# Weights times values with the values stationary in the two column halves of TensorE, weights normalized before the transposes, and all scores in native float32

## Chip, core and metric

The kernel runs on one NeuronCore of one Trainium2 chip. The metric is device time in microseconds (us) of one execution. TensorE (PE) multiplies, VectorE (DVE) and ScalarE (ACT) do everything that is done element by element, GpSimd (POOL) prepares a few constants, and SyncE (SP) issues the loads and stores. PEld is the row of the profile for the loading of stationary operands into PE.

## What is computed

Local attention with a few global keys, then two feed-forward layers on its result:

```python
scores = scale * np.matmul(q, k.transpose(0, 1, 3, 2))        # batch 2, heads 8, seq 768, head_dim 64
is_global = pos[None, :] < int(n_global)                      # n_global 8
is_local = (rel >= 0) & (rel < int(n_local))                  # n_local 96
scores = np.where(keep, scores + bias, -1000000000.0)         # bias: -slope of the head * distance
a = np.exp(scores - np.max(scores, axis=-1, keepdims=True))
a = a / (np.sum(a, axis=-1, keepdims=True) + 1e-09)
x = np.matmul(a, v)                                           # to 1536 tokens x 512
x = moe(x)     # h = x @ w_in (512 x 2048), ELU of h, @ w_out (2048 x 512)
return moe2(x) # the same sizes, h * sigmoid(1.702 h)
```

## The kernel before

**Rows and units.** The 1536 tokens are 12 rows of 128 queries, 6 in each batch. A row is worked in two units of 4 heads, so there are 24 units. The queries of a row look at one block of 128 keys (the first row of a batch) or at two: its own block, and the block before it, whose first 32 keys are overwritten with the first 32 keys of the batch, so that the global keys lie there (`load_va` for the values, the copies at the end of the scores in `unit` for the keys).

**One unit** (`Band.unit`, lines 585 to 735) runs so:
- Scores on PE (L627), head pairs in the two row halves of the array, since a head has 64 dimensions. Rows 0 to 3 are native float32 (`NNAT = 4`; row 0's are issued at L281). From row 4 on q and k are split into a high and a low part of a shorter float (`prep`, L555: two copies and two subtractions of 128x512 each row), and three matmuls hi*hi, hi*lo, lo*hi add up to a score block. From row 4 on the scores of both units are made at once (`WHOLE = 4`).
- DVE adds the distance and takes the row's extreme (L658), ACT takes exp in place (L662) into `E`.
- PE transposes the 4 blocks (one a head and key block) of `E` (L675), and ACT or DVE copies them to `pt` (L681).
- PE multiplies: `pt` is stationary (128 keys x 128 queries), `v` with two further columns of ones is streamed (66 columns, L692). So `ob` holds, with queries on the partitions, 64 values and the sum of the weights.
- DVE adds 1e-9 to the sums (L703), takes reciprocals (L705) and scales (L707) into `o`.
- PE transposes `o` back (L718), so that features are on the partitions, into `xb`. After the second unit ACT and DVE write the row's `xh` (L731) and `xl` (L734), the split input of the first layer.

**The layers** (`FFN`) work in 8 groups of 4 blocks of 128 hidden units, for each of 3 chunks of 512 tokens: `A` (L397, first product, then the activation on ACT and DVE and a split into `g`), `B` (L437, second product, added to `acc` or `d`). Each product is three matmuls of split operands, too. `conv` turns the weights, which arrive as float32, into split operands (L362 to L374). The first group's first chunk is worked as two halves of 256 tokens, so that it can start when rows 0 and 1 are done.

**What sets the order.** `Plan` is a list scheduler that runs when the program is built. Every step is a node with a due time, the engines that it can run on with a planned cost, and the buffers it reads and writes. `TIMES` sets the due times of the units, `LEAD`, `CONV0` and `CONVS` those of the layers and conversions. Steps with two possible engines are given to the one that is planned to end first. Where PE is planned to be idle before 45 us, `idle` puts matmuls on zeros of 256 columns there (L747), "fill" from here on. There are 8 banks of PSUM, allotted by the plan too.

**The beginning** (`start`, `load`): SP loads the two sizes `n_raw`, then q and k of row 0 in two halves, row 1, and v of row 0. `NWARM = 8` matmuls of 512 zero columns run on PE meanwhile (L278).

Of the kernel before, what the change touches and what calls it, by code (L numbers as in the profile page):

```python
# [19 lines left out]
NB = S // 128  # L20
# [7 lines left out]
LEAD = 9.86  # L28
CONV0 = (-15.923, 4.66)
CONVS = (-57.99, -6.01)  # L30
TIMES = (8.0, 3.97, 3.55)
NWARM = 8
START = dict(PE=6.3, ACT=5.4, DVE=5.6, POOL=5.9, SP=5.9)
WARM = 5.0
SLOW = 8.0
ROW0 = 5.6, 6.3
PEEK = 0.58, 3.0
FILL = 45.0
NNAT = 4
WHOLE = 4  # L40
NGBUF = 5
# [4 lines left out]
VW = D + 2  # L46
# [20 lines left out]
class Node:  # L67
    __slots__ = ("due", "opts", "npred", "succ", "ready", "alloc", "uses")
# [13 lines left out]
class Plan:  # L82
# [18 lines left out]
    def node(self, due, opts, reads=(), writes=(), alloc=None, uses=()):  # L101
        n = Node()
        alloc = [] if alloc is None else alloc if isinstance(alloc, list) else [alloc]
        n.due, n.opts, n.alloc, n.uses = due, opts, alloc, uses
# [144 lines left out]
def start(k, ns, load):  # L249
# [12 lines left out]
    V.memset(f32(k.zero), 0.0)  # L262
    rel, neg = (k.e[0][:, x:x + 256] for x in (0, 256))
# [5 lines left out]
                   allow_small_or_imprecise_dtypes=True)  # L269
    k.ident = cp.tile([128, 128], F32, name="ident")  # L270
    make_identity(nc, k.ident)
    for t in k.v + k.va:
        nc.gpsimd.memset(t[:, :, D:VW], 1.0)
# [9 lines left out]
    small = lambda n, nm, dt=F32: cp.tile([128, n], dt, name=nm)  # L283
# [7 lines left out]
    V.tensor_scalar(a[:, 0:1], k.ng, float(NGLOB), None, ALU.is_le)  # L291
    V.tensor_scalar(a[:, 1:2], k.nl, float(NWIN + 1), None, ALU.is_le)
    V.tensor_scalar(k.big, col, k.ng, BIG, ALU.is_ge, ALU.mult)
    V.scalar_tensor_tensor(c, k.nl, 1.0, a[:, 1:2], ALU.is_ge, ALU.mult)
    V.scalar_tensor_tensor(w, rel[:, 128:256], k.nl, k.big, ALU.is_ge, ALU.mult)
    V.tensor_tensor(flag, c, a[:, 0:1], ALU.mult)
# [8 lines left out]
class FFN:  # L305
# [23 lines left out]
    def gbuf(self, i):  # L329
        if i < 4:  # L330
            return [(self.k.g[:, 2 * i + x, :], [("g", i, x)]) for x in range(2)]
        return [(self.k.q[1][x].rearrange("p a b -> p (a b)"), [("q", 1, x)]) for x in range(2)]
# [43 lines left out]
    def A(self, due, G, c, f, t0=0, n=TC):  # L376
# [6 lines left out]
        i = self.nA % 4 if self.nA < 12 else self.nA % NGBUF  # L383
# [115 lines left out]
class Band:  # L499
# [6 lines left out]
    def __init__(self, k, plan, pool):  # L506
# [3 lines left out]
        self.E = k.E  # L510
        self.pt = [t([128, 512], F32, f"pt{i}") for i in range(4)]
        self.o = [t([128, 512], F32, f"o{i}") for i in range(2)]
# [23 lines left out]
    def load(self, r, due):  # L536
        k, node = self.k, self.plan.node
        p = r % 2
        if r < 2:
            self.plan.given((4.9, 7.6)[r], ("acc", 0, r), *(("kn", pr, r) for pr in range(NP)))  # L540
        if r == 0:
            self.plan.given(9.3, ("v", 0))
# [3 lines left out]
        elif r >= NNAT:  # L546
            node(due, [("SP", 0.33, lambda: k.load_qk(r), 1.7)], writes=["rqk"])
        if r > 0:
            node(due + 0.1, [("SP", 0.6, lambda: k.load_v(r, self.v[p][:, :, 0:D]), 1.4)],
                 writes=[("v", p)])  # L550
        if r % NB:
            node(due + 0.2, [("SP", 1.3, lambda: k.load_va(r, self.va[p][:, :, 0:D]), 1.4)],
                 writes=[("va", p)])

    def prep(self, r, due):  # L555

        k, nc, node = self.k, self.k.nc, self.plan.node
        i = r % NB
        pos, p = POS[i], r % 2
        if r < NNAT:  # L560
            return
        if r == NNAT:
            for a, b, x in ((0, NGLOB, 0), (NGLOB, 128, 3)):
                src = k.kn[:, x, :, a:b]
                h, l = (k.kT[:, y, :, a:b] for y in range(2))
                n = NP * (b - a)
                kn = [("kn", pr, x) for pr in range(NP)]
                key = [[("kT", y, pr, 0) for pr in range(NP)] for y in range(2)]
                x = node(due - 2, o_copy(k, h, src, n), kn, key[0])
                x.ready = dict.fromkeys(ENGINES, 20.0)  # L570
                node(due - 1.5, o_sub(k, l, src, f32(h), n), kn + key[0], key[1])
        qh, ql = k.q[p]
        node(due, o_copy(k, qh, k.rqk[:, 0], 512), ["rqk"], [("q", p, 0)])
        node(due + 0.5, o_sub(k, ql, k.rqk[:, 0], f32(qh), 512), ["rqk", ("q", p, 0)], [("q", p, 1)])
        kb = lambda x, ps: [("kT", x, pr, ps) for pr in range(NP)]
        kh, kl = (k.kT[:, x, :, pos * 128:(pos + 1) * 128] for x in range(2))
        node(due + 0.2, o_copy(k, kh, k.rqk[:, 1], 512), ["rqk"], kb(0, pos))
        node(due + 1, o_sub(k, kl, k.rqk[:, 1], f32(kh), 512), ["rqk"] + kb(0, pos), kb(1, pos))
        if i == 3:
            for x in range(2):  # L580
                node(due + 1.5, o_copy(k, k.kT[:, x, :, 32:128],
                                       f32(k.kT[:, x, :, 3 * 128 + 32:4 * 128]), 384),
                     kb(x, 3), kb(x, 0))

    def unit(self, u, due):
# [6 lines left out]
        pos = POS[i]  # L592
        c0 = (pos + 1) * 128 - W
        q = k.q[p]
# [4 lines left out]
        native = r < NNAT  # L599
# [397 lines left out]
```

## Time and profile before

| | us |
|---|---|
| median of 3 runs | 623.6 (623.06 to 623.67) |
| the profiled execution | 623.17 |
| its span, first to last instruction | 621.4 |
| PE busy in the span | 614.6 (99%), 3257 records |
| DVE busy | 407.1 (66%) |
| ACT busy | 319.3 (51%) |
| granted TensorE clock, mean | 0.999 of full speed |

1.8 us of the profiled execution lie around the span. "Busy" is the time in which an engine has an instruction under way; on PE, where matmuls are pipelined and their ends are modelled, the distance from one start to the next says more of what a matmul costs, and the timeline of PE shows it: a line of the timeline is a run of like instructions, with the start of the first. A native float32 matmul leaves two records in the trace, any other one.

### The profile page before, as it was taken

To read this page: it belongs to the slowest core of one execution; us is meant where nothing else is said; L and a number is where in the kernel's file an instruction comes from. 1 tells how busy PE (TensorE), PEld (TensorE's weight loads), DVE (VectorE), ACT (ScalarE), POOL (GpSimd) and SP (SyncE) were. 2 spreads that over 40 slices of the span, in tenths; PEclk is the share of its full clock that TensorE was granted. 3 is DMA by queue.
4 is the path that set the end of the run, shared out by engine and by line. 5 is a ranking of instruction groups with operands and counts; after the bars stand their busy time and mean duration, and the time that the engine had idled before them with its cause. 6 is when DMAs were issued, how large, how long until landed. Compare 5 with 4: busy or idle time off the path is not lost.

```text
span 621.4 us, 8504 instructions
## 1 busy us (share of the span) xinstructions
PE 614.6 (99%) x3257; PEld 520.9 (84%) x3257; DVE 407.1 (66%) x873; ACT 319.3 (51%) x612; POOL 1.4 (0%) x12
## 2 busy tenths in 40 slices
PE   8999999999999999999999999999999999999997
PEld 6899998888888888888888888888888888888886
DVE  7999996737844687459856984188347954654433
ACT  6998887846724653444654654356115422521320
POOL 0000000000000000000000000000000000000000
PEclk9999999999999999999999999999999999999999
DMA  7766461212310032012210221023101310101012
GB/s 220 233 183 214 119 190 35 55 49 69 136 69 0 35 135 103 0 35 102 102 34 1 102 101 69 1 102 136 35 0 69 135 69 0 35 0 52 17 69 73
DMA packets 36833, 49.39 MB, mean 79 GB/s; under 512 B 24624, under 2 KB 25392, under 8 KB 36784
## 3 DMA queue, kind: packets, MB, share of 16 engines
q1 hardware_dynamic: 36784, 48.77, 24.2%
q8 instruction: 27, 0.44, 0.3%
q14 instruction: 22, 0.18, 0.1%
HBM read 45.62 MB, written 3.15 MB: 78 GB/s over the span
## 4 chain that ended last, share of the span: by engine, by line
PE 98%; DMA 1%; SPq 0%; DVE 0%; issue 0%
PE bank L397 42%; PE bank L437 42%; PE bank L692 6%; PE bank L675 3%; PE bank L627 3%; DMA acc<-in_qk_dram 1%; PE bank L718 1%; SPq L904 0%; DVE d L458 0%; SPq L259 0%
## 5 line engine op out<-in xcount | busy, mean ns | idle before, releaser
L397 PE MATMUL bank<-xh,wbig 128*128 128x512 f32 (+1 forms) x560 | 174.6, 381 | 0.0
L397 PEld LDWEIGHTS bank<-xh,wbig 128*128 128x128 f32 x560 | 103.9, 188 | 18.7
L397 PE MATMUL bank<-xl,wbig 128*128 128x512 f32 (+1 forms) x280 | 105.5, 377 | 0.0
L437 PE MATMUL bank<-g,wbig 128*128 128x512 f32 (+1 forms) x420 | 96.8, 369 | 0.0
L437 PEld LDWEIGHTS bank<-g,wbig 128*128 128x128 f32 x420 | 73.1, 188 | 12.4
L397 PE MATMUL bank<-xh,kT 128*128 128x512 f32 x240 | 76.3, 389 | 0.0
L241 DVE TENSOR_TENSOR g<-gt,g 128x512 fp32r<-128x512 f32 (+1 forms) x82 | 54.5, 665 | 26.2 <-ACT g L234 24.9
L234 ACT ACTIVATE g<-gt 128x512 fp32r<-128x512 f32 (+1 forms) x82 | 50.1, 611 | 40.8 <-DVE gt L415 24.9
L437 PE MATMUL bank<-wbig,g 128*128 128x512 f32 (+1 forms) x267 | 67.5, 387 | 0.0
L458 DVE SCALAR_TENSOR_TENSOR acc<-bank,acc 128x512 f32<-128x512 f32 x48 | 33.2, 692 | 52.2 <-PE bank L437 52.0
L413 ACT ACTIVATE e<-bank 128x512 f32<-128x512 f32 x48 | 28.6, 597 | 69.4 <-PE bank L397 69.1
L397 PEld LDWEIGHTS bank<-xl,wbig 128*128 128x128 f32 x280 | 52.7, 188 | 9.1
L437 PEld LDWEIGHTS bank<-wbig,g 128*128 128x128 f32 x267 | 49.8, 188 | 10.2
L234 ACT ACTIVATE wbig<-m 128x512 fp32r<-128x512 f32 x41 | 26.0, 634 | 59.8 <-PE bank L397 36.4
L397 PEld LDWEIGHTS bank<-xh,kT 128*128 128x128 f32 x240 | 45.0, 188 | 9.3
L415 DVE SCALAR_TENSOR_TENSOR gt<-e,bank 128x512 f32<-128x512 f32 x48 | 32.9, 685 | 29.7 <-ACT e L413 29.4
L437 PE MATMUL bank<-kT,g 128*128 128x512 f32 (+1 forms) x198 | 49.6, 383 | 0.0
L364 ACT ACTIVATE m<-raw 128x512 f32<-128x512 f32 x61 | 40.6, 666 | 12.5 <-DMA raw<-in_w2i_dram 6.2
L397 PE MATMUL bank<-xl,kT 128*128 128x512 f32 x120 | 46.7, 389 | 0.0
L410 DVE SCALAR_TENSOR_TENSOR gt<-e,bank 128x512 f32<-128x512 f32 (+1 forms) x52 | 33.5, 644 | 17.8 <-ACT e L408 16.9
L371 DVE SCALAR_TENSOR_TENSOR m<-m,raw 128x512 int32<-128x512 int32 x64 | 44.0, 688 | 0.8
L369 DVE SCALAR_TENSOR_TENSOR raw<-raw 128x512 int32<-128x512 int32 x64 | 44.0, 688 | 0.6
(118 smaller groups left out, 858.8 us busy)
## 6 DMA issues: line engine op xcount, KB each, us to landing
raw<-in_w1i_dram SPq DMA_DIRECT2D x16, 512.0 KB, 3.3
raw<-in_w1o_dram SPq DMA_DIRECT2D x16, 512.0 KB, 3.2
raw<-in_w2i_dram SPq DMA_DIRECT2D x16, 512.0 KB, 3.2
raw<-in_w2o_dram SPq DMA_DIRECT2D x16, 512.0 KB, 3.2
rqk<-in_qk_dram SPq DMA_DIRECT2D x8, 512.0 KB, 4.2
v<-in_v_dram SPq DMA_DIRECT2D x12, 256.0 KB, 3.9
out_dram<-acc SPq DMA_DIRECT2D x8, 256.0 KB, 2.0
va<-in_v_dram SPq DMA_DIRECT2D x10, 192.0 KB, 4.3
```

The source lines that it names most:

```text
L234: ("ACT", n / 1200 + (0.05 if psum else 0.09), lambda: nc.scalar.activation(out, in_, AF.Copy)),
L241: return [("DVE", n / 960 + 0.068, lambda: nc.vector.tensor_tensor(out, a, b, ALU.subtract))]
L364: ("ACT", 0.52, lambda: nc.scalar.activation(mf, topf, AF.Copy, scale=sc)),
L369: node(due + 1, [("DVE", 0.6, lambda: V.scalar_tensor_tensor(top, bot, 29, top, ALU.logical_shift_right, ALU.bitwise_or))], [kr], [kr])
L371: node(due + 1.5, [("DVE", 0.6, lambda: V.scalar_tensor_tensor(m, m, 3, top, ALU.logical_shift_left, ALU.bitwise_or))], [km, kr], [km])
L397: nc.tensor.matmul(h(), lhsT=w[:, kk, :], rhs=x[:, kk, :], start=(kk == 0 and j == 0), stop=(kk == KK - 1 and j == 2))
L410: node(due + 1, [("DVE", n / 960 + 0.07, lambda: V.scalar_tensor_tensor(gt, e, -1.0, h(), ALU.add, ALU.max))], [ke, b], [kg], uses=[b])
L413: node(due, [("ACT", n / 1200 + 0.05, lambda: S.activation(e, h(), AF.Tanh, scale=0.851))], [b], [ke], uses=[b])
L415: node(due + 1, [("DVE", n / 960 + 0.07, lambda: V.scalar_tensor_tensor(gt, e, 1.0, h(), ALU.add, ALU.mult))], [ke, b], [kg], uses=[b])
L437: nc.tensor.matmul(o(), lhsT=lhsT, rhs=rhs, start=(f == 0 and j == 0), stop=(f == GF - 1 and j == 2))
L458: node(due, [("DVE", n / 960 + 0.07, lambda: V.scalar_tensor_tensor(acc, o(), sc, acc, ALU.mult, ALU.add))], [b] + ka, ka, uses=[b])
L692: nc.tensor.matmul(ob.tile[:, n * VW:(n + 1) * VW], lhsT=pt[:, (hd * nw + ch) * 128:(hd * nw + ch + 1) * 128], rhs=v[:, 4 * half + n, :], ...
```

## The change

- **Weights times values:** `v` (64 columns of a head) is stationary, `pt` (128 queries) is streamed. Head 0 of a pair goes to the left 64 columns of the array and partitions 0 to 63 of PSUM, head 1 to the right half and partitions 64 to 127. The result has the features on the partitions and goes to `xb` at once; the transposes of `o`, `o` itself and the two columns of ones in `v` are gone.
- **Sums and normalization:** exp on ACT also gives the sum (`accum_out`). DVE adds 1e-9, takes reciprocals, and scales the four blocks of `E` before they are transposed.
- **Scores:** all rows are native float32, in matmuls of 128 columns for each key block (rows 1 to 3 had 256 columns). `prep` is gone; q and k of rows 4 to 11 lie in three buffers `qk`. Rows 4 to 7 make their scores unit by unit now (`WHOLE = 8`).
- **The beginning:** the halves of rows 0 and 1 are issued on the ACT and SP queues, 6 zero matmuls instead of 8, the flag that picks the program is worked out earlier.
- **The plan:** other due times and costs, a reserve of PSUM banks (`spare`), six `g` buffers instead of five.

```diff
-LEAD = 9.86
-CONV0 = (-15.923, 4.66)
-CONVS = (-57.99, -6.01)
-TIMES = (8.0, 3.97, 3.55)
-NWARM = 8
+LEAD = 13.8
+CONV0 = (-12.46, 4.78)
+CONVS = (-57.99, -1.63)
+TIMES = (8.0, 4.6, 3.75)
+NWARM = 6
...
-WHOLE = 4
-NGBUF = 5
+WHOLE = 8
+NGBUF = 6
...
-                    self.banks) >= len(n.alloc) else 1e9
+                    self.banks) >= len(n.alloc) + n.spare else 1e9
...
-    for t in k.v + k.va:
-        nc.gpsimd.memset(t[:, :, D:VW], 1.0)
...
             def mm():
                 for y, pr in enumerate(ps):
-                    js = slice(y % 2 * W, (y % 2 + 1) * W)
-                    for n, (a, x) in enumerate(parts):
+                    for w, (keys, _) in enumerate(blocks):
+                        js = slice(y % 2 * W + w * 128, y % 2 * W + w * 128 + 128)
                         for hd in range(2):
                             rows = slice(64 * hd, 64 * hd + 64)
-                            rhs = (k.kn[rows, pos + 1 - nw:pos + 1, pr, :] if native
-                                   else x[rows, pr, c0:c0 + W])
-                            nc.tensor.matmul(own[y // 2 * 2 + hd].tile[:, js], lhsT=a[rows, pr, :],
-                                             rhs=rhs, start=(n == 0), stop=(n == len(parts) - 1))
+                            nc.tensor.matmul(own[y // 2 * 2 + hd].tile[:, js], lhsT=q[rows, pr, :],
+                                             rhs=keys[rows, pr, :], start=True, stop=True)
...
-                node(at + 0.5, [("ACT", W / 1200 + 0.19, lambda n=n, e=e: nc.scalar.activation(
-                    e, e, AF.Exp, bias=st[:, n:n + 1], scale=-1.0))],
-                    [(kE, n), (kst, n)], [(kE, n)])
-        ob = Bank()
+                node(at + 0.5, [("ACT", W / 1200 + 0.28, lambda n=n, e=e: nc.scalar.activation(
+                    e, e, AF.Exp, bias=st[:, n:n + 1], scale=-1.0, accum_out=st[:, 4 + n:5 + n]))],
+                    [(kE, n), (kst, n)], [(kE, n), (kst, 4 + n)])
+        node(due + 2.1, [("DVE", 0.17, lambda: V.tensor_scalar(
+            st[:, 8:12], st[:, 4:8], 1e-9, None, ALU.add))],
+            [(kst, 4 + n) for n in range(4)], [(kst, 8)])
+        node(due + 2.2, [("DVE", 0.1, lambda: V.reciprocal(st[:, 12:16], st[:, 8:12]))],
+             [(kst, 8)], [(kst, 12)])
+        for n in range(4):
+            e = E[:, n, 0:W]
+            node(due + 2.3, o_ts(k, e, e, st[:, 12 + n:13 + n], 1.0, ALU.mult, ALU.mult, W),
+                 [(kE, n), (kst, 12)], [(kE, n)])
...
             def pv(j=j, pt=pt):
-                for hd in range(2):
-                    n = 2 * j + hd
-                    for ch in range(nw):
-                        v = self.v[p] if ch == nw - 1 else self.va[p]
+                pr = 2 * half + j
+                for ch in range(nw):
+                    v = self.v[p] if ch == nw - 1 else self.va[p]
+                    for hd in range(2):
                         nc.tensor.matmul(
-                            ob.tile[:, n * VW:(n + 1) * VW],
-                            lhsT=pt[:, (hd * nw + ch) * 128:(hd * nw + ch + 1) * 128],
-                            rhs=v[:, 4 * half + n, :], start=(ch == 0), stop=(ch == nw - 1))
+                            xb.tile[64 * hd:64 * hd + 64, pr * 128:(pr + 1) * 128],
+                            lhsT=v[:, 2 * pr + hd, :],
+                            rhs=pt[:, (hd * nw + ch) * 128:(hd * nw + ch + 1) * 128],
+                            start=(ch == 0), stop=(ch == nw - 1))
...
-        def ot():
-            for j in range(2):
-                n = 2 * half + j
-                nc.tensor.transpose(xb.tile[:, n * 128:(n + 1) * 128], o[:, n * 128:(n + 1) * 128],
-                                    k.ident)
...
     def load():
-        load_early(0, 2)
-        load_early(1)
-        load_v(0, k.v[0][:, :, 0:D])
+        for r in range(2):
+            load_early(r, (nc.scalar, nc.sync))
+        load_v(0, k.v[0])
```

**How rows move.** Names are buffers with a number; L692 and L718 of before are the product and the transposes of `o`, L664 of the change is the product, L675 and L647 are the transposes of `E`, L627 and L596 the scores, L747 and L697 the fill matmuls. On PE in the middle of the third row (two key blocks), before:

```order
L627 MATMUL bank_70<-acc 128x256
L692 MATMUL bank_68<-va_104,pt_180 128x66
L692 MATMUL bank_68<-v_102,pt_180 128x66
L692 MATMUL bank_68<-va_104,pt_180 128x66
L692 MATMUL bank_68<-v_102,pt_180 128x66
L718 MATMUL bank_71<-ident,o_182 128x128 x2
L692 MATMUL bank_68<-va_104,pt_181 128x66
```

and with the change, in the second row:

```order
L596 MATMUL bank_68<-acc 128x128
L664 MATMUL bank_66<-pt_177,va_105 64x128 x2
L664 MATMUL bank_66<-pt_177,v_103 64x128 x2
L664 MATMUL bank_66<-pt_178,va_105 64x128 x2
L664 MATMUL bank_66<-pt_178,v_103 64x128 x2
L647 MATMUL bank_73<-ident,E_99 128x128 x4
L647 MATMUL bank_69<-ident,E_99 128x128 x4
L697 MATMUL bank_67<-q1h 128x256 x5
```

The transposes of `o` between the products are gone, two heads stand in one row as a pair of matmuls (x2), and fill matmuls have come in.

On PE at the beginning, from the first fill matmul on, before:

```order
L747 MATMUL bank_70<-q1h 128x256 x5
L627 MATMUL bank_70<-acc 128x256
L627 MATMUL bank_71<-acc 128x256
L627 MATMUL bank_70<-acc 128x256
L627 MATMUL bank_71<-acc 128x256
L675 MATMUL bank_72<-ident,E_99 128x128 x2
```

and with the change, behind row 1's scores, of which the last is the first row here:

```order
L596 MATMUL bank_73<-acc 128x128
L697 MATMUL bank_66<-q1h 128x256 x7
L647 MATMUL bank_66<-ident,E_99 128x128 x2
L647 MATMUL bank_67<-ident,E_99 128x128 x2
L697 MATMUL bank_69<-q1h 128x256 x3
L664 MATMUL bank_69<-pt_177,v_102 64x128 x2
L664 MATMUL bank_69<-pt_178,v_102 64x128 x2
L697 MATMUL bank_68<-q1h 128x256 x20
```

Both units' scores of row 1 stand ahead of the first transposes, and in all there are 40 fill matmuls where there were 5.

On DVE at the end of the second unit, before (the sums come out of PSUM, L703, and the scaled result goes to `o`, L707):

```order
L703 TENSOR_SCALAR st_185<-bank_70 128x4
L705 RECIPROCAL st_185<-st_185 128x4
L707 TENSOR_TENSOR o_182<-bank_70,st_185 128x256
L367 TENSOR_SCALAR raw_90<-raw_90 128x512
L369 SCALAR_TENSOR_TENSOR raw_90<-raw_90 128x512
```

and with the change, at the third unit (L626 to L629 sums and reciprocals, L245 the scaling of `E`, L619 the scores' minimum):

```order
L626 TENSOR_SCALAR st_183<-st_183 128x4
L629 RECIPROCAL st_183<-st_183 128x4
L234 COPY acc<-acc 128x2x32
L245 TENSOR_SCALAR E_101<-E_101,st_183 128x256 x4
L619 ISA E_100,st_182<-bank_68,d 128x256
```

The normalization stands ahead of the transposes now, and takes four instructions of 256 columns instead of one.

## Rows read from the trace of the kernel before

**Rows 1.** The page: busy time by engine, and the chain that ended last.

```profile
PE 614.6 (99%) x3257; PEld 520.9 (84%) x3257; DVE 407.1 (66%) x873; ACT 319.3 (51%) x612; POOL 1.4 (0%) x12
...
PE 98%; DMA 1%; SPq 0%; DVE 0%; issue 0%
```

**Rows 2.** Windows: length, busy us (instructions) of PE, PEld, DVE, ACT, POOL; clock; DMA.

```profile
16.00:32.00 16.00, 16.00 (x139) 14.28 (x138) 15.90 (x53) 15.79 (x38) 0.00 (x0) 1.00 0.75 226
32.00:48.00 16.00, 16.00 (x150) 15.57 (x149) 15.80 (x56) 16.00 (x40) 0.00 (x0) 1.00 0.70 198
...
64.00:80.00 16.00, 16.00 (x163) 15.56 (x162) 14.55 (x61) 13.09 (x37) 0.00 (x0) 1.00 0.40 116
...
200.00:400.00 200.00, 200.00 (x884) 165.62 (x883) 131.98 (x211) 101.30 (x168) 0.00 (x0) 1.00 0.18 64
```

**Rows 3.** Groups by shape on PE: the products and the transposes of `o`.

```profile
L692 PE MATMUL bank<-v,pt 128*128 128x66 f32 x192 | 35.0, 275 | 0.0
L692 PE MATMUL bank<-va,pt 128*128 128x66 f32 x160 | 29.8, 268 | 0.0
...
L718 PE MATMUL bank<-ident,o 128*128 128x128 f32 x48 | 9.5, 279 | 0.0
```

**Rows 4.** Timeline of PE, rows 2 and 3: start, us, line, tiles, shape, count.

```profile
17.25 2.00 PE L627 MATMUL bank<-acc 64*128 64x256 f32 x16
19.18 0.44 PE L718 MATMUL bank<-ident,o 128*128 128x128 f32 x2
...
22.02 0.60 PE L675 MATMUL bank<-ident,E 128*128 128x128 f32 x4
22.55 1.13 PE L627 MATMUL bank<-acc 64*128 64x256 f32 x8
23.61 0.44 PE L692 MATMUL bank<-va,pt 128*128 128x66 f32 x2
...
24.33 0.39 PE L692 MATMUL bank<-v,pt 128*128 128x66 f32 x2
24.56 0.39 PE L718 MATMUL bank<-ident,o 128*128 128x128 f32 x2
24.78 0.34 PE L692 MATMUL bank<-va,pt 128*128 128x66 f32 x2
```

**Rows 5.** Timeline of PE: split scores of row 4, 24 matmuls between these starts.

```profile
37.01 0.50 PE L627 MATMUL bank<-kT,q0h 64*128 64x256 f32 x4
...
38.63 0.66 PE L675 MATMUL bank<-ident,E 128*128 128x128 f32 x4
```

**Rows 6.** Timelines of PE at the beginning, three windows; in brackets idle before.

```profile
5.84 0.72 PE L281 MATMUL bank<-acc 64*128 64x128 f32 x10
...
6.07 0.50 PE L281 MATMUL bank<-acc 64*128 64x128 f32 x6
...
6.49 0.86 PE L747 MATMUL bank<-q1h 128*128 128x256 f32 x5
8.62 1.14 PE L627 MATMUL bank<-acc 64*128 64x256 f32 x8 [1.26 <-DMA acc<-in_qk_dram]
```

**Rows 7.** Timeline of DVE: scaling, subtraction of a split, and the score step.

```profile
7.87 0.89 DVE L246 TENSOR_SCALAR d<-gt 128x256 f32<-128x256 f32 x4
8.68 0.28 DVE L658 CUSTOM_DVE_ANT_0 E<-bank,E 128x128 f32<-128x128 f32 x1
...
17.91 0.69 DVE L241 TENSOR_TENSOR wbig<-m,wbig 128x512 fp32r<-128x512 f32 x1
18.51 0.42 DVE L707 TENSOR_TENSOR o<-bank,st 128x256 f32<-128x256 f32 x1
18.85 0.42 DVE L658 CUSTOM_DVE_ANT_0 E<-bank,d 128x256 f32<-128x256 f32 x1
```

**Rows 8.** Groups by shape on DVE: reading out an accumulator.

```profile
L658 DVE DVE_READ_ACCUMULATOR2_ANT st<- 128x1 f32 x96 | 8.0, 83 | 0.0
```

More of the change, by code (lines that the diff above doesn't have):

```diff
@@ L27 @@
 NSLOT = 6
-LEAD = 9.86
-CONV0 = (-15.923, 4.66)
-CONVS = (-57.99, -6.01)
-TIMES = (8.0, 3.97, 3.55)
-NWARM = 8
-START = dict(PE=6.3, ACT=5.4, DVE=5.6, POOL=5.9, SP=5.9)
+LEAD = 13.8
[3 more added lines that the diff above has]
+NWARM = 6
+START = dict(PE=5.8, ACT=5.1, DVE=5.9, POOL=5.9, SP=5.6)
 WARM = 5.0
 SLOW = 8.0
-ROW0 = 5.6, 6.3
-PEEK = 0.58, 3.0
+ROW0 = 5.2, 5.8
+PEEK = 0.47, 3.0
 FILL = 45.0
 NNAT = 4
-WHOLE = 4
-NGBUF = 5
+WHOLE = 8
+NGBUF = 6
 NG = DFF // 128 // GF
@@ L331, in gbuf @@
             return [(self.k.g[:, 2 * i + x, :], [("g", i, x)]) for x in range(2)]
-        return [(self.k.q[1][x].rearrange("p a b -> p (a b)"), [("q", 1, x)]) for x in range(2)]
+        return [(self.k.q[i - 4][x].rearrange("p a b -> p (a b)"), [("q", i - 4, x)])
+                for x in range(2)]
     def acc(self, c, m):
@@ L510, in __init__ @@
         self.E = k.E
+        k.qk = [k.rqk] + [t([128, 2, NP, 128], F32, f"qk{i}") for i in range(1, 3)]
         self.pt = [t([128, 512], F32, f"pt{i}") for i in range(4)]
[L512 removed]
         self.st = [t([128, 16], F32, f"st{i}") for i in range(3)]
@@ L539, in load @@
         if r < 2:
-            self.plan.given((4.9, 7.6)[r], ("acc", 0, r), *(("kn", pr, r) for pr in range(NP)))
+            self.plan.given((4.4, 6.0)[r], ("acc", 0, r), *(("kn", pr, r) for pr in range(NP)))
         if r == 0:
-            self.plan.given(9.3, ("v", 0))
+            self.plan.given(8.8, ("v", 0))
+            self.plan.given(5.35, "d0")
         if 1 < r < NNAT:
@@ L553, in load, with keys @@
                  writes=[("va", p)])
[L555 to L559, printed above, removed]
+    def keys(self, r):
+        k = self.k
         if r < NNAT:
[L561 to L583, printed above, removed]
@@ L585, in unit @@
+            return k.kn[:, r], [("kn", pr, r) for pr in range(NP)]
+        return k.qk[r % 3][:, 1], [("k", r % 3, pr) for pr in range(NP)]
     def unit(self, u, due):
@@ L619, in mm @@
+            blocks = [self.keys(x) for x in range(r + 1 - nw, r + 1)]
+            kk = [kq] + [names[pr] for _, names in blocks for pr in ps]
             def mm():
                 for y, pr in enumerate(ps):
-                    js = slice(y % 2 * W, (y % 2 + 1) * W)
-                    for n, (a, x) in enumerate(parts):
+                    for w, (keys, _) in enumerate(blocks):
+                        js = slice(y % 2 * W + w * 128, y % 2 * W + w * 128 + 128)
                         for hd in range(2):
@@ L896, in tile_local_attention_two_ffn, with load_qk, load_early @@
     k.rqk = t([128, 2, NP, 128], F32, "rqk")
-    def load_qk(r):
-        nc.sync.dma_start(out=k.rqk, in_=qk[r])
-    def load_early(r, n=1):
-        w = 512 // n
-        for c in (slice(j * w, j * w + w) for j in range(n)):
-            nc.sync.dma_start(out=k.acc[:, r::NNAT, c],
-                              in_=qk[r].rearrange("p x a b -> p x (a b)")[:, :, c])
+    def load_qk(r, to=None):
+        nc.sync.dma_start(out=k.rqk if to is None else to, in_=qk[r])
+    def load_early(r, queues=(nc.sync,)):
+        w = 512 // len(queues)
+        for j, queue in enumerate(queues):
+            c = slice(j * w, j * w + w)
+            queue.dma_start(out=k.acc[:, r::NNAT, c],
+                            in_=qk[r].rearrange("p x a b -> p x (a b)")[:, :, c])
     heads = lambda a: a.rearrange("p (h d) -> p h d", d=D)
```

90 lines of the change are left out of this document (30 added, 60 removed).

## Prediction

> **What bounds the kernel now.** I read the page first: PE is busy for 99% of the span, and the chain that ended last runs over PE for 98% [rows 1]. That alone proves little, since a busy PE need not be a dense one, so I then read the timeline of PE for the distances between starts. They are constant: every two records of the product take 0.22 to 0.23 us, also where another line follows [rows 4]. Only ahead of the first scores of row 1 is there a wait, 1.26 us for their load [rows 6]. The windows say what would come next: from 16 to 48 us DVE and ACT are as full as PE (15.9 and 15.8 of 16, then 15.8 and 16.0), from 64 us on both have slack, and in the layers, 200 to 400 us, DVE is busy 132 of 200 us and PE 200 [rows 2]. So a microsecond taken off PE is a microsecond of the end, except in about the first 70 us, where DVE and ACT may not let PE run ahead.
>
> The sum is made against the profiled execution, 623.2 us; the median of the runs is 0.4 us above it, less than I can resolve.
>
> **The products, the large term.** A float32 matmul leaves two records; 192 and 160 records [rows 3] are 176 matmuls. A record takes 0.112 us from start to start (24.33 to 24.56) [rows 4], so the products take 352 x 0.112 = 39.4 us. A record streams 66 columns there, but a transpose of 128 columns takes the same 0.11 (24.56 to 24.78, two of them), so it isn't the streaming that sets the pace; both load 128 stationary columns. With the change a record streams 128 columns and loads 64. No row shows two matmuls in the two column halves. The nearest show two in the row halves, float32 as well: 10 records from 5.84 on and 6 from 6.07 on, so 4 records or two pairs in 0.23 us [rows 6], 0.115 a pair at 128 columns; at 256 columns 16 records take 1.93 us with what follows, 8 take 1.06 [rows 4], so four pairs take 0.87, 0.109 for each 128 columns. Were the two row halves not at work at once, a pair would take twice that. So the bounds for a pair of records in the column halves are 0.112 (at once) and 0.223 (one after the other). I take 0.112, from the row halves: 176 x 0.112 = 19.7 us, a gain of **19.7 us**; the other end is no gain.
>
> **The change of array shape.** Going into and out of the row halves costs time: of the 1.06 us of four pairs 0.87 are streaming, so 0.19 is not; and four transposes ahead of them take 0.53 us (22.02 to 22.55) where four take 4 x 0.11 = 0.44 [rows 4]. Together 0.28 us a group. By the order the products stand in 27 groups, with other work between. Whether the column halves cost this too no row shows; bounds 0 and 0.28. I take 0.28, the only row of such a change: **+7.6 us**; the other end is 0. The Trainium skill says that changing the tiling mode drains TensorE (TensorEngine Tiling (Array Packing), Key Properties); the 0.28 us of the row halves agree with it, and by the rule the column halves would pay as well, so 615; without it 607.
>
> **The transposes of o** go: 48 [rows 3] at 0.11 us: **-5.3 us**.
>
> **The scores.** Row 4's 24 split matmuls take 38.63 - 37.01 = 1.62 us [rows 5]. Native in 128 columns they are 16 pairs of records: 16 x 0.112 + 0.28 = 2.07 us. Rows 8 to 11: 4 x 0.45 = 1.8. Rows 4, 5 and 7 make two groups each: 2 x (0.90 + 0.28) - 1.62 = 0.74, so 2.2. Row 6 (one key block) and rows 1 to 3 (8 pairs of 128 columns for 4 of 256, the same streaming) I put at 0.3 together. Sum **+4.3 us**.
>
> **The beginning.** Row 1 is issued on two queues and lands earlier: the wait of 1.26 us [rows 6] can go. Two zero matmuls fewer, but the load of row 0 sets that start: I take 0.4 (0 to 0.9). Sum **-1.7 us**.
>
> **Idle PE early.** Before the first layer has work, PE has rows 0 to 3 only, and DVE and ACT are full there [rows 2]. Per unit of two key blocks the change adds four scalings, 0.2 us each (four in 0.81, 7.87 to 8.68), and takes away one of 0.34 (18.51 to 18.85) [rows 7]; ACT gets four sums to read out, for which the nearest row is DVE's accumulator, 0.083 us each [rows 8], where it hides nearly all behind the next instruction; bounds 0 and 0.2. For rows 0 to 3: 24 x 0.2 + 8 x 0.13 + 32 x 0.08 - 8 x 0.34 = 5.7 us on two engines that were full, about 3 us each, while PE loses work. For rows 4 to 6 the split of q and k goes, two subtractions of 0.60 (17.91 to 18.51) [rows 7] and two copies, about 2.1 us a row, which pays for the scalings there. So PE must wait early. How much, the order says in part: 40 fill matmuls where 5 stood, 35 x 0.12 = **+4.2 us**; for 256 columns in one record I take the pace of the split scores, (1.62 - 0.28) / 12 = 0.11 us a pair [rows 5], rounded up. Beyond the fill I put **+2 us** for waits on DVE and ACT up to row 6 (0 to 7). Later both have room (64 to 80) [rows 2], and what was hidden stays so. Loads of v as plain rows, the three qk buffers, POOL's constants and the sixth g buffer cost nothing: no wait on them but the one of 1.26 us ends on PE.
>
> **Sum:** -19.7 + 7.6 - 5.3 + 4.3 - 1.7 + 4.2 + 2.0 = -8.6, so 623.2 - 8.6 = 614.6. I say **614.5 us**.
>
> **Rivals.**
> 1. *DVE and ACT bind the first 70 us.* If the sums cost ACT 0.2 us each, 56 of them up to row 6 cost 11 us instead of 4.6, and the chain of each unit (four exps, sum, reciprocal, scalings, only then transposes) leaves holes on two full engines: waits of 7 instead of 2 us, **619.5 us** (618 to 623). For it: [rows 2]; against it: the split of rows 4 to 6 leaves the same engines.
> 2. *The column halves don't run at once.* Then the product keeps 0.223 us a pair: no 19.7, and all other terms stay but the 2 us of waits, since PE is slower: -5.3 + 4.3 + 7.6 - 1.7 + 4.2 = +9.1, **632 us**, slower than before. It decides where a pair costs over 0.112 + 8.6 / 176 = 0.16 us. It is also the case in which the change doesn't do what it says; that the transposes and the split are gone and the matmuls stand in pairs the order shows. Against it: the row halves run at once in float32 [rows 4, 6]. The Trainium skill (TensorE: Matmul & The Clock Gate, Part 3, The mechanism) says that a weight load overlaps running matmuls only when their row groups differ; the column halves share all rows, so by that sentence loads would stand between the matmuls and this rival holds. The trace doesn't bear it out as a general rule: in the layers all matmuls use all rows, and loads are busy 166 of 200 us while PE is never idle [rows 2].
> 3. *The change of shape is free* for column halves, and the waits stay small: 614.5 - 7.6 = **607 us**.
>
> **How the numbers follow.** Forecast, 608 to 618: 0.71. Rival 1: 0.13, of which 0.04 (from 622 on) lie within 0.2% of before. Rival 2: 0.08. Rival 3, below 608: 0.08. About 0.2% (1.2 us) is what a measurement of this kernel can tell from no change. Faster: 0.71 + 0.08 + 0.09 = 0.88; same 0.04; slower 0.08. The range holds the forecast, all but the end of rival 1, and the start of rival 3: 607 to 621.5.
>
> **What would show it.** The products: pairs of L664 records a few ns apart and 0.11 us from pair to pair; 0.22 means rival 2. The shape: distances of about 0.3 us between the last matmul of a product group and the next line; 0.11 to 0.12 means rival 3. Scores of rows 8 to 11 of 2.1 us. PE's starts with holes before about 75 us, ended by ACT or DVE, and none behind; the sixth row should be done by 75 us or so. The layers must keep their pace, some 884 records in 200 us. The prediction is wrong if PE waits behind 80 us too, or if the clock, full throughout before [rows 2], falls in the early holes to the lower of its two levels (1.2 of 2.4 GHz), which would double the time of what PE does there.

## The result, and the profile after

| | before | changed |
|---|---|---|
| median, us | 623.33 (623.03 to 623.67) | 617.35 (616.78 to 618.49) |
| ratio | | 0.9904, 95% interval 0.9893 to 0.9916 |
| profiled execution, its span | 623.17, 621.4 | 617.15, 615.3 |

The kernel became 1.0% faster. The forecast was 614.5 us, 2.9 below the median, and the time lies in its range. The page of the changed kernel, busy time by engine and the chain that ended last, against [rows 1]:

```profile
PE 606.0 (98%) x3338; PEld 503.2 (82%) x3338; DVE 410.1 (67%) x921; ACT 318.1 (52%) x694; POOL 1.2 (0%) x10
...
PE 92%; DVE 5%; ACT 1%; DMA 1%; issue 0%
```

Six parts in a hundred of the chain have left PE. The windows say where, with the columns of [rows 2]:

```profile
16.00:32.00 16.00, 15.46 (x181) 13.12 (x179) 15.96 (x66) 15.69 (x50) 0.00 (x0) 1.00 0.63 228
32.00:48.00 16.00, 15.93 (x173) 14.29 (x169) 15.96 (x57) 15.93 (x51) 0.00 (x0) 1.00 0.43 134
48.00:64.00 16.00, 14.76 (x132) 13.35 (x132) 15.28 (x45) 13.51 (x39) 0.00 (x0) 1.00 0.49 159
64.00:80.00 16.00, 16.00 (x170) 14.29 (x169) 15.59 (x69) 14.56 (x54) 0.00 (x0) 1.00 0.55 170
200.00:400.00 200.00, 200.00 (x884) 165.62 (x883) 134.41 (x217) 101.58 (x172) 0.00 (x0) 1.00 0.19 64
```

DVE is full to 15.96 of 16 from 16 to 48 us, and PE has holes up to 64 us. From there on PE is full, and the layers keep their 884 records in 200 us.

I added up the distances from each record of PE to the next, by the kind of the first (waits count with the record ahead of them):

| kind, us of PE | before | changed | difference |
|---|---|---|---|
| products | 37.9 | 24.6 | -13.4 |
| transposes of `o` | 4.6 | 0 | -4.6 |
| scores | 20.4 | 23.6 | +3.3 |
| transposes of `E` | 18.3 | 20.6 | +2.4 |
| zero matmuls and fill | 5.8 | 10.1 | +4.2 |
| layers | 528.6 | 529.5 | +0.9 |
| from the last matmul's start to the end | 4.4 | 5.5 | +1.1 |
| sum | | | -6.1 |

The timeline of PE (start, us, line, tiles, shape, count) shows products between scores and transposes, against [rows 4]:

```profile
19.04 1.16 PE L596 MATMUL bank<-acc 64*128 64x128 f32 x16
20.13 0.44 PE L664 MATMUL bank<-pt,va 128*64 128x128 f32 x4
20.40 0.39 PE L664 MATMUL bank<-pt,v 128*64 128x128 f32 x4
20.62 0.39 PE L664 MATMUL bank<-pt,va 128*64 128x128 f32 x4
20.84 0.39 PE L664 MATMUL bank<-pt,v 128*64 128x128 f32 x4
21.16 1.09 PE L647 MATMUL bank<-ident,E 128*128 128x128 f32 x8
```

Four records, two pairs, take 0.22 us (20.40 to 20.62): the two heads are at work at once. The way out takes 0.10 more (20.84 to 21.16 is 0.32), the way in 0.05 (20.13 to 20.40) plus 0.09 at the record ahead, together 0.245 a group on average. All 27 groups show the same, beside the waits. Three of these, from the same view:

```profile
23.07 0.44 PE L664 MATMUL bank<-pt,va 128*64 128x128 f32 x4 [0.23 <-ACT pt L653]
...
31.59 0.44 PE L664 MATMUL bank<-pt,va 128*64 128x128 f32 x4 [0.31 <-ACT pt L653]
...
54.21 1.23 PE L647 MATMUL bank<-ident,E 128*128 128x128 f32 x8 [1.08 <-DVE E L245]
```

The one at 54.21 waits for the scaling of `E`. The groups by shape of the two new element-by-element steps (busy us, mean ns):

```profile
L245 DVE TENSOR_SCALAR E<-E,st 128x256 f32<-128x256 f32 x80 | 22.8, 348 | 0.5
...
L623 ACT ACTIVATION_READ_ACCUMULATOR E<-E,st 128x1 f32 x96 | 18.6, 193 | 0.0
```

### The profile page after: what moved, and what is told of

Read it like the earlier page. It is cut to its first block, busy times and chain, and to the rows that moved or that the text cites. A ratio compares the mean times of both kernels' runs of the same rounds, so it can differ in the third digit from the quotient of the medians.

```text
span 615.3 us, 8766 instructions
## 1 busy us (share of the span) xinstructions
PE 606.0 (98%) x3338; PEld 503.2 (82%) x3338; DVE 410.1 (67%) x921; ACT 318.1 (52%) x694; POOL 1.2 (0%) x10
## 4 chain that ended last, share of the span: by engine, by line
PE 92%; DVE 5%; ACT 1%; DMA 1%; issue 0%
PE bank L437 43%; PE bank L397 41%; PE bank L596 3%; PE bank L664 2%; PE bank L647 2%; DVE E L245 1%; DVE E L619 1%; PE bank L697 1%; DMA acc<-in_qk_dram 1%; ACT E L623 1%; DVE xl L684 0%; DVE wbig L240 0%; DVE m L371 0%; DVE raw L369 0%; ACT pt L653 0%; DVE raw L367 0%
## 5 line engine op out<-in xcount | busy, mean ns | idle before, releaser
L397 PE MATMUL bank<-xh,wbig 128*128 128x512 f32 (+1 forms) x560 | 172.6, 380 | 0.1
L437 PE MATMUL bank<-g,wbig 128*128 128x512 f32 (+1 forms) x360 | 80.6, 367 | 0.2 <-DVE xl L684 0.2
L397 PE MATMUL bank<-xh,kT 128*128 128x512 f32 x240 | 78.3, 392 | 0.0
L437 PEld LDWEIGHTS bank<-g,wbig 128*128 128x128 f32 x360 | 62.5, 188 | 11.9 <-DVE xl L684 0.4
L240 DVE TENSOR_TENSOR g<-gt,g 128x512 fp32r<-128x512 f32 (+1 forms) x70 | 46.4, 663 | 20.6 <-ACT g L233 19.5
L437 PE MATMUL bank<-wbig,g 128*128 128x512 f32 (+1 forms) x246 | 59.8, 384 | 0.0
L233 ACT ACTIVATE g<-gt 128x512 fp32r<-128x512 f32 (+1 forms) x70 | 42.6, 609 | 24.7 <-DVE gt L415 15.2
L437 PEld LDWEIGHTS bank<-wbig,g 128*128 128x128 f32 x246 | 45.4, 188 | 9.1
L623 ACT ACTIVATE E<-E,st 128x256 f32<-128x256 f32 (+1 forms) x96 | 46.0, 484 | 1.7 <-DVE st L619 1.6
L364 ACT ACTIVATE m<-raw 128x512 f32<-128x512 f32 x58 | 38.6, 666 | 14.5 <-DMA raw<-in_w2i_dram 6.1
```

The source lines that it names most:

```text
L233: ("ACT", n / 1200 + (0.05 if psum else 0.09), lambda: nc.scalar.activation(out, in_, AF.Copy)),
L240: return [("DVE", n / 960 + 0.068, lambda: nc.vector.tensor_tensor(out, a, b, ALU.subtract))]
L364: ("ACT", 0.52, lambda: nc.scalar.activation(mf, topf, AF.Copy, scale=sc)),
L397: nc.tensor.matmul(h(), lhsT=w[:, kk, :], rhs=x[:, kk, :], start=(kk == 0 and j == 0), stop=(kk == KK - 1 and j == 2))
L437: nc.tensor.matmul(o(), lhsT=lhsT, rhs=rhs, start=(f == 0 and j == 0), stop=(f == GF - 1 and j == 2))
L623: node(at + 0.5, [("ACT", W / 1200 + 0.28, lambda n=n, e=e: nc.scalar.activation(e, e, AF.Exp, bias=st[:, n:n + 1], scale=-1.0, accum_out= ...
```

## Experiments

Times are medians with lowest and highest, ratios are to the kernel before on the same chip.

**Are the halves at once, and what does a change of shape cost?** One kernel puts both heads of a pair into the same half, pairs alternating between the halves:

```diff
-                for ch in range(nw):
-                    v = self.v[p] if ch == nw - 1 else self.va[p]
-                    for hd in range(2):
+                for hd in range(2):
+                    for ch in range(nw):
+                        v = self.v[p] if ch == nw - 1 else self.va[p]
...
-                            xb.tile[64 * hd:64 * hd + 64, pr * 128:(pr + 1) * 128],
+                        at, ps = 64 * (pr % 2), 2 * (pr // 2) + hd
...
+                            xb.tile[at:at + 64, ps * 128:(ps + 1) * 128],
```

> The changed kernel (617.35 us), but both heads of a pair use the same column half, pairs alternate between the halves, and a head's key blocks stand together; the rows of the first layer's weights are laid out to fit, so the result is the same. Theory (the gain of the product comes from two halves at work at once): a float32 record of 128 columns then costs 0.11 us alone, 352 x 0.11 = 38.7 us where 19.4 were, so +19.3, less up to 3 us that PE waited anyway: 633 us (630 to 637). Rival (the gain comes from loading 64 stationary columns instead of 128): no more than 1 us off, 617 to 618.

628.65 us (627.97 to 629.73), ratio 1.0083 (1.0062 to 1.0104). Timeline of PE, L665 is the product here:

```profile
21.88 0.43 PE L665 MATMUL bank<-pt,va 128*64 128x128 f32 x2
22.15 0.38 PE L665 MATMUL bank<-pt,v 128*64 128x128 f32 x2
22.37 0.44 PE L665 MATMUL bank<-pt,va 128*64 128x128 f32 x4
22.59 0.44 PE L665 MATMUL bank<-pt,v 128*64 128x128 f32 x4
```

Within a half a pair of records takes 0.22 us (22.15 to 22.37), twice the time of a pair in the changed kernel. Products take 35.4 us of PE instead of 24.6. It did not come to 633, since where one pair ends and the next begins, in the other half, the two overlap (the lines with x4). The rival, that loading 64 stationary columns instead of 128 is what gives the gain (617 to 618), falls: a record alone in its half takes 0.11 us with 64 as it did with 128.

The second keeps the heads in their two halves, but takes head 0's matmuls first, then head 1's (the first half of the diff above alone):

> The changed kernel with one edit: in rows with two key blocks the two matmuls of head 0 (left half) come first, then the two of head 1 (right half), instead of alternating. Theory (matmuls are taken in order, so halves overlap only where neighbours lie in different halves): of 8 records in a pair of heads some 6 or 7 stand one after the other where 4 pairs stood, so 0.66 to 0.77 us for 0.44; 40 such groups: +9 to +13 us, less up to 3 us of waits, 624 to 630. Rival (the queue finds work for the idle half by itself): within 1 us of 617.

618.1 us (617.58 to 618.92), ratio 0.991 (0.9893 to 0.9928). My theory, that neighbours in one half must wait for one another, fell:

```profile
21.82 0.45 PE L664 MATMUL bank<-pt,va 128*64 128x128 f32 x4
22.09 0.40 PE L664 MATMUL bank<-pt,v 128*64 128x128 f32 x4
22.31 0.44 PE L664 MATMUL bank<-pt,va 128*64 128x128 f32 x4
22.53 0.44 PE L664 MATMUL bank<-pt,v 128*64 128x128 f32 x4
```

The program has `va`, `v` of head 0 and then `va`, `v` of head 1, but the trace shows both heads' `va` records side by side, 13 ns apart, then both heads' `v`. Each half went its own way, two matmuls ahead of the program's order; the halves are at once, and the order within a group costs nothing that these times can tell.

The third makes the stationary operand 128 columns wide, both heads' values at once, so that no shape changes (of each pair of heads only one result is left, the other is overwritten):

> Both heads' 64 columns are loaded together as 128 stationary columns, so the array's shape doesn't change for the product; the two heads of a pair are written over each other, so one of them is lost from the result. A record costs 0.11 us as in the kernel before, 352 x 0.11 = 39 us, and the changes of shape in and out of the 27 product groups fall away. Theory (a change of shape costs about 0.25 us a group): 6 to 7 us less than the run with one half, so 626 to 628. Rival (what shows at the groups' borders is the latency of any first matmul): equal to the run with one half within 1.5 us.

630.27 us (630.13 to 630.38), ratio 1.0107 (1.009 to 1.0124).

```profile
21.95 0.49 PE L664 MATMUL bank<-pt,va 128*128 128x128 f32 x2
22.28 0.39 PE L664 MATMUL bank<-pt,v 128*128 128x128 f32 x2
22.50 0.39 PE L664 MATMUL bank<-pt,va 128*128 128x128 f32 x2
```

A record takes 0.112 us, as in before [rows 4], though it streams 128 columns and not 66. Products: 39.5 us, against 352 x 0.055 = 19.4 at the pace of the halves, so 20.1 us more. The span is 13.2 us longer (628.5), of which 1.6 is its beginning (first transposes at 11.55 instead of 10.00, see the last part below). So what is absent here is worth 20.1 - 11.6 = 8.5 us: 27 changes of shape, by the distances above 27 x 0.245 = 6.6, and 0.7 of waits; 1.2 I did not take apart.

**The idle time of PE early.** Without the fill matmuls, in the same order:

```diff
-FILL = 45.0
+FILL = 0.0
```

> The changed kernel without its 40 fill matmuls, everything else in the same order. Theory (PE would stand idle there, waiting for DVE and ACT): within 1 us of 617.35. Rival 1 (the fill stands in the way of real work): up to 4 us faster, 613.5. Rival 2 (without the fill the clock falls to 1.2 GHz in the first 35 us): slower by some microseconds, granted clock below 1.0 in the windows up to 32 us.

617.79 us (616.78 to 618.36), ratio 0.9906 (0.9886 to 0.9926): no difference to the changed kernel that these times can tell. The fill covers idle time and neither costs nor saves. Windows with PE, PEld, DVE, ACT, POOL, clock:

```profile
8.00:16.00 8.00, 6.32 (x56) 5.23 (x54) 6.99 (x44) 7.29 (x32) 0.00 (x0) 0.91 0.93 308
16.00:24.00 8.00, 6.95 (x74) 5.70 (x72) 7.65 (x32) 7.18 (x26) 0.00 (x0) 0.88 0.66 259
```

The view has the granted clock at 0.91 and 0.88 on average there, with PE idle 1.7 and 1.0 of 8 us, and it cost no time that the end shows.

Without the 96 scalings (the weights stay unnormalized), the order planned anew:

```diff
-        for n in range(4):
-            e = E[:, n, 0:W]
-            node(due + 2.3, o_ts(k, e, e, st[:, 12 + n:13 + n], 1.0, ALU.mult, ALU.mult, W),
-                 [(kE, n), (kst, 12)], [(kE, n)])
```

> The changed kernel without the 96 scalings of E on DVE (0.26 us each in its trace, 24 us in all), so the weights aren't normalized; the order around them is planned anew (23 fill matmuls instead of 40). Theory (DVE and ACT bind PE up to about 56 us, which cost 4 us of fill and 2.7 us of waits): PE becomes dense earlier and the end comes 3 to 6 us sooner, 611.5 to 614.5. Rival (the early waits are the latency of the loads and of the first units, not DVE's work): no more than 1 us off 617.35.

616.53 us (614.58 to 618.07), ratio 0.9885 (0.9854 to 0.9917). The wait at 54.21 is gone, and from 10 to 90 us PE's timeline names no wait at all, but 23 fill matmuls remain. By the medians the scalings cost 0.8 us, less than I expected and not clear of noise, since the two ratios' intervals overlap. The profiled execution shows the slow beginning of the last part below, so the true price may be up to 2.8 us (616.16 against the 618.92 of the kernel with heads one after the other, whose slow beginning lasts 1.3 us longer); by the lowest times of both kernels it is 2.2 (614.58 against 616.78).

The same scalings, planned at the 0.26 us that they took instead of 0.20. The work stays, and the plan changes: the order, with it the engine of a few steps, and 56 fill matmuls instead of 40:

```diff
-            node(due + 2.3, o_ts(k, e, e, st[:, 12 + n:13 + n], 1.0, ALU.mult, ALU.mult, W),
+            node(due + 2.3, [("DVE", W / 1920 + 0.13, lambda e=e, n=n: V.tensor_scalar(
+                e, e, st[:, 12 + n:13 + n], 1.0, ALU.mult, ALU.mult))],
```

> The changed kernel, with the planned cost of a scaling set to what the trace shows (0.26 us for 256 columns instead of 0.20); only the order changes. If the wait of 1.3 us for the scaling at 52.9 us and its like come from a plan that counts DVE too cheap: 615.5 to 616.5. If DVE's and ACT's work decides, whatever the order: 616.8 to 618.

622.18 us (621.68 to 622.75), ratio 0.9976 (0.9967 to 0.9986): nearly 5 us lost by the plan alone, or 4 against the 618.1 of the kernel with heads one after the other, whose profile has a like beginning. Timeline of PE, the waits from 48 to 64 us:

```profile
51.61 1.23 PE L649 MATMUL bank<-ident,E 128*128 128x128 f32 x8 [0.34 <-DVE E L634]
...
53.47 0.98 PE L437 MATMUL bank<-g,wbig 128*128 128x256 f32 x6 [0.63 <-ACT pt L655]
...
56.40 1.23 PE L649 MATMUL bank<-ident,E 128*128 128x128 f32 x8 [0.93 <-DVE E L634]
```

With the due times chosen anew for that cost (`LEAD`, `CONV0`, `TIMES`, `WHOLE`; the diff is those numbers):

> The planned cost of a scaling set to the 0.26 us measured (as in the kernel that came to 622.2), and then the due times chosen anew for that cost (LEAD 12.99, CONV0 -7.11 and 4.22, TIMES 8.0, 4.6, 3.53, WHOLE 6); the same work in another order, 49 fill matmuls. Theory (the 5 us lost there were due times that no longer fitted the planned costs, and can be had back): 617.5 to 619.5 us, waits of PE at 50 to 61 us below 1.5 in sum. Rival (an honest cost makes no better order, the order of the changed kernel is good by trial): 621 us or more.

618.86 us (618.61 to 620.11), ratio 0.9932 (0.9911 to 0.9952), with PE busy 15.78 of 16 us from 48 to 64. So 3.3 us of the loss were due times that no longer fitted the planned costs, though the truer cost has made no better plan than the 617.35 us of the changed kernel. What the early part costs is set by the order as much as by the sums of work.

71 of the scalings moved to GpSimd, as a second engine that the plan may choose:

> The changed kernel, with GpSimd as a second engine for the scalings at a planned 0.73 us for 256 columns; the plan gives it 71 of the 96. Theory (DVE's work binds the first 56 us): if GpSimd keeps about the planned cost and doesn't slow DVE, 612 to 615. Rival (GpSimd is slower or takes time from DVE, and the scaling now stands longer in the chain of a unit): 618 or more.

619.45 us (618.38 to 619.86), ratio 0.9935 (0.9915 to 0.9954). DVE remained as full, 15.89 of 16 us from 16 to 32, and GpSimd took 0.63 us for one (6.93 us for 11). No gain; the rival (618 or more) holds.

Rows 0 to 3 with the product of before, rows 4 to 11 with the new one:

> Rows 0 to 3 work as in the kernel before (weights stationary, ones in v, scaling of 64 columns after the product, transposes of o), rows 4 to 11 as with the change. DVE has some 5 us less to do in the first rows, ACT 3 us; PE gets 6.2 us of products and 1.8 us of transposes more, 2.5 us fewer changes of shape and 29 fill matmuls (3.4 us) less. Theory (in the first rows DVE and ACT set the time, PE has room): 613.5 to 616.5. Rival (PE's own sum decides): 617.35 + 2 = 619.5.

618.68 us (617.01 to 619.07), ratio 0.9922 (0.9903 to 0.9941). Fill fell to 11 matmuls, and the waits that PE's timeline names from 10 to 90 us to 0.8 us in sum (1.8 in the changed kernel), yet the time is no better: what PE no longer waited, it spent on the old products and transposes. So the idle time of the first rows was not worth avoiding in this way; the rival of PE's sum (619.5) came closer than my theory.

The old product in all rows, the rest of the change kept:

> The changed kernel with the product of before for all rows: pt stationary, v with two columns of ones streamed, sums from the product, transposes of o back; the sums of exp and the scalings of E are left out. What stays of the change is the native scores, the loads, the beginning and a new order. Theory (the terms add up): before 623.3, plus 3.5 for the native scores with their changes of array shape, minus 1.3 for the beginning, plus 0.8 for 7 more fill matmuls: 626 to 627 us, products 37.9 us of PE again, transposes of o 4.6. Rival (the split of q and k, gone for rows 4 to 11, frees DVE and ACT so much that PE's scores cost nothing): 622 us or less, with no waits on DVE or ACT before 60 us.

634.73 us (632.45 to 637.0), ratio 1.0168 (1.0127 to 1.0209), 8 us above what I expected. This one decides nothing: the buffers of `o` lie where q and k of every third row are loaded, so from row 6 on part of these is overwritten, and loads, scalings into `o` and its transposes can wait for each other. PE waits 3.10 us for a scaling into `o` ahead of 88.23 us, and from 88 to 96 us the granted clock is 0.57. What the native scores are worth by themselves stays open.

**The beginning.** The kernel before with the new loads and the six zero matmuls alone:

```diff
-NWARM = 8
+NWARM = 6
...
-        load_early(0, 2)
-        load_early(1)
+        for r in range(2):
+            load_early(r, (nc.scalar, nc.sync))
```

> The kernel before with the new beginning alone: the halves of rows 0 and 1 on the ACT and SP queues, 6 zero matmuls instead of 8; the order of all else as before. Theory: the wait of 1.26 us ahead of row 1's scores goes, and nothing else moves: 622.0 us (621.6 to 622.4). Rival: what is late next (DVE's distances, the first exps) takes its place, 623.3 us. On the tail: if the last store lands later in the changed kernel because of the change, the tail here stays at 4.3 us from the last matmul's start; if it varies from run to run, it can be 5 here too.

623.86 us (622.73 to 624.35), ratio 1.0002 (0.9991 to 1.0012). The wait of 1.26 us [rows 6] is gone, and yet nothing is gained. Timeline of PE:

```profile
1.45 2.93 PE L278 MATMUL bank<-q1h 128*128 128x512 f32 x6 [1.45 <-DVE q1h L262]
5.05 2.08 PE L281 MATMUL bank<-acc 64*128 64x128 f32 x16 [0.67 <-DMA acc<-in_qk_dram]
7.06 1.43 PE L747 MATMUL bank<-q1h 128*128 128x256 f32 x5
8.42 2.08 PE L627 MATMUL bank<-acc 64*128 64x256 f32 x8
10.43 0.86 PE L675 MATMUL bank<-ident,E 128*128 128x128 f32 x4
```

The five fill matmuls took 1.43 us where they took 0.86, the eight records of scores 2.08 where they took 1.14 [rows 6]: PE ran at about half its pace until 10 us or so, and the first transposes stand 0.74 us later than in before (9.69). The windows' clock column (the first of the last three) does not show it:

```profile
6.00:8.00 2.00, 2.00 (x16) 1.78 (x13) 1.93 (x12) 2.00 (x9) 0.00 (x0) 1.00 1.05 224
8.00:10.00 2.00, 2.00 (x11) 1.38 (x9) 1.74 (x13) 2.00 (x8) 0.00 (x0) 1.00 1.00 210
```

The reason lies in the view. The trace's record of the granted clock begins only with the rise to the upper level, at 10.91 us here and at 5.69 in the kernel before, and the column counts as 1.00 what stands ahead of it.

So I looked at this stretch in the other profiles. The changed kernel, and then the one with heads one after the other:

```profile
5.07 1.47 PE L282 MATMUL bank<-acc 64*128 64x128 f32 x16 [0.68 <-DMA acc<-in_qk_dram]
6.58 0.38 PE L697 MATMUL bank<-q1h 128*128 128x256 f32 x1
6.88 2.06 PE L596 MATMUL bank<-acc 64*128 64x128 f32 x32
8.87 1.10 PE L697 MATMUL bank<-q1h 128*128 128x256 f32 x7
10.00 0.82 PE L647 MATMUL bank<-ident,E 128*128 128x128 f32 x4
```

```profile
5.04 2.08 PE L282 MATMUL bank<-acc 64*128 64x128 f32 x16 [0.66 <-DMA acc<-in_qk_dram]
7.05 0.58 PE L697 MATMUL bank<-q1h 128*128 128x256 f32 x1
7.56 3.60 PE L596 MATMUL bank<-acc 64*128 64x128 f32 x32
11.09 1.09 PE L697 MATMUL bank<-q1h 128*128 128x256 f32 x7
12.02 0.60 PE L647 MATMUL bank<-ident,E 128*128 128x128 f32 x4
```

The work is the same, the first transposes stand 2.02 us apart, and the spans 1.8 (617.1 against 615.3). Of the 12 profiles with six zero matmuls, 9 show the low pace in row 0's scores (2.08 us), 3 the full one (1.47). The clock records agree: they begin at 4.59, 4.73 and 4.99 us in the three (4.59 is the changed kernel), and between 8.63 and 13.97 in the nine (10.84 with one head after the other). So the changed kernel with 8 zero matmuls:

```diff
-NWARM = 6
+NWARM = 8
```

> The changed kernel with 8 zero matmuls at the beginning again instead of 6; nothing else is touched. In the changed kernel's profile the 16 records of row 0's scores take 1.47 us and the first transposes start at 10.00; with the heads taken one after the other, the same order of work, they took 2.08 us and the first transposes started at 12.02, and PE came to its full pace only behind them. Theory (the two zero matmuls, 0.85 us of PE, were what kept PE from idling for 0.68 us ahead of row 0's scores, and with them PE is at full pace from those scores on in every run): row 0's scores in about 1.4 to 1.5 us, first transposes at 10.0 to 10.2, all timed runs within 1 us of each other around 616.8 us. Rival (the pace of the beginning is chance, whatever stands ahead): timed runs spread from 616.5 to 618.7 as before.

617.02 us (616.93 to 617.37), ratio 0.9891 (0.9875 to 0.9908). Timeline of PE:

```profile
1.46 3.78 PE L279 MATMUL bank<-q1h 128*128 128x512 f32 x8 [1.46 <-DVE q1h L261]
5.17 1.25 PE L282 MATMUL bank<-acc 64*128 64x128 f32 x16
6.46 0.38 PE L697 MATMUL bank<-q1h 128*128 128x256 f32 x1
6.77 2.06 PE L596 MATMUL bank<-acc 64*128 64x128 f32 x32
```

There is no gap ahead of row 0's scores, the clock record begins at 5.14 us, the pace is full from there, and the four times lie within 0.44 us of each other where those of the changed kernel spread over 1.71. That agrees with my theory and doesn't show it. The kernel before, with eight zero matmuls too, has the early rise as well, but two profiles can be chance where 3 of 12 rise early in spite of the gap. The narrow spread says little: the kernel with full-width operands and six zero matmuls lies within 0.25 us, and the kernel before spread over 1.76 on the chip of this run. The median with eight is 0.3 us below that of the changed kernel, which is less than can be told apart; it is the lowest of the kernels that do all the work.

## Why the prediction was right, point by point

- **Products, -19.7: right.** Pairs take 0.11 us, 352 x 0.055 = 19.4 us in all, against 37.9: -18.5. The bound taken from the row halves was the true one; rival 2 fell with the first experiment, where one half alone takes 0.22 a pair. The Trainium skill (TensorE: Matmul & The Clock Gate, Part 3, The mechanism) says that a weight load overlaps running matmuls only when their row groups differ; the trace doesn't bear that out as a general rule, since the column halves share all rows and a pair still takes 0.11 us.
- **Change of shape, +7.6: right, a little too large.** 27 x 0.245 = 6.6 us. Rival 3 falls. The Trainium skill says that a change of the tiling mode drains TensorE (TensorEngine Tiling (Array Packing), Key Properties); the trace agrees, with 0.245 us a group.
- **Transposes of `o`, -5.3:** -4.6.
- **Scores, +4.3:** +3.3. Whole groups of rows 8 to 11 take 1.99 us, 0.37 more than the split ones (1.62), where I took 0.45; the half groups of rows 4, 5 and 7 take 1.09, 0.56 a row more, where I took 0.74. I charged the way into the row halves (0.09 at the record ahead) to the native scores alone, but the split ones lie in the row halves too and paid it as well, ahead of their start. Rows 0 to 3 and 6 came to 0.15 instead of 0.3.
- **The beginning, -1.7: the number came true by luck.** Row 1's scores start at 6.88 instead of 8.62. The wait of 1.26 is gone, as forecast. But the two zero matmuls fewer, for which I took 0.4, brought 0.1 (row 0's scores start at 5.07, and with eight zero matmuls at 5.17 in both kernels); the number is right since four of the five fill matmuls that stood there, 0.5 us, stand elsewhere, and these the fill counts already. And the profile is one of the three with the early rise of the clock. The zero matmuls filled PE up to row 0's scores; without them PE stands idle for 0.68 us, and in 9 of 12 profiles the low pace lasted until 8.6 us or later. That can take back the whole gain, as the kernel before with the new beginning showed.
- **Fill, +4.2: right.** 40 x 0.12 = 4.8 instead of 0.6.
- **Waits beyond the fill, +2 (0 to 7): right in size, with more in small pieces.** The long distance ahead of 54.21 has 1.16 us more than a change of shape explains, those ahead of 23.07 and 31.59 some 0.3 and 0.4, and one for `xl` 0.16: 2.0. The releasers are the ones named, DVE's scaling and ACT's copies. A scaling took 0.263 us from start to start where I took 0.2: the row behind my figure [rows 7] scaled by a constant into another buffer, and these scale by a column of scalars in place. A sum of exp took ACT 0.095 (16.93 to 17.02 in its timeline) where I took 0.08, not the 0.2 of rival 1, and that rival's 7 us of waits did not come. The scalings make 24 x 0.063 = 1.5 us more work on a full DVE up to row 3. That those two engines bind there is shown by the windows and by the chain, most of whose pieces from 15.9 to 55.6 us lie on them. That the scalings alone were the cause is not: taking them away ended the waits, but gave 0.8 us by the medians, and at most 2.8.
- **Not foreseen: the end, +1.1.** From the last matmul's start to the end the kernel before had 4.35 us, the changed kernel 5.48. All of it lies behind the issue of the last store (3.5, then 4.6 us). Before's order with the new beginning has 4.44, the other variants 4.7 to 5.6. Nothing in these stores was changed; the cause stays open.

By these terms -18.5 + 6.6 - 4.6 + 3.3 - 1.7 + 4.2 + 2.0 + 1.1 = -7.6, where the span fell by 6.1. Of the 1.5 left over 0.5 are the fill matmuls that the beginning and the fill both count; 1.0 I did not take apart. So the mechanism held, and the 2.9 us between forecast and median are no single step: products (1.2) and transposes of `o` (0.7) gave less than forecast, the end took 1.1 more, and scores and change of shape, 1.0 less each, made part of it good.

## What to carry to other kernels

Two heads of 64 dimensions can share TensorE in the two column halves at full pace each; count the changes of shape (0.245 us a group here) and put work of one shape together. When work moves onto engines that are full, the order decides what it costs: choose due times anew after any change of a planned cost, since the plan alone moved the time by 4 to 5 us here. Before a zero matmul at the beginning is removed, look for the gap that it covers, and at more than one profile.

## What the runs showed of the hardware

- The two column halves run apart from each other: with the heads one after the other in the program, the trace has their records side by side, 13 and 96 ns apart.
- TensorE starts at the lower of its two levels: the zero matmuls of 512 columns stand 0.427 us apart, 1.2 columns a nanosecond or 1.2 GHz, while the granted clock reads 1.00, since its record begins with the rise. When the pace rises differs between profiles with the same work up to row 0's scores (4.59 to 4.99 us in three, 8.63 to 13.97 in nine). What matmuls take there has to be read from their starts. The Trainium skill (TensorE: Matmul & The Clock Gate, Part 1: The HAM clock gate (the "warmup" mystery)) says that the number of matmuls at the lower level varies from run to run; the nine and three profiles agree.
- Native float32 with a full-width stationary operand takes 0.112 us a record with 66 columns streamed [rows 4] and with 128 alike; in one column half alone, with 64 stationary columns, 0.109.
- A scaling by a column of scalars in place, 128x256, takes DVE 0.263 us (four in 1.05, 15.76 to 16.81 in DVE's timeline), and GpSimd 0.63; one by a constant into another buffer takes DVE 0.20 [rows 7].
